# A kernel that plans its own instruction order: new figures in the planner of a fused attention and feed-forward kernel

## The chip, the core and the metric

The kernel runs on one core of a Trainium2 chip. A core has TensorE (matmuls, PE in the profile; its weight loads are PEld), VectorE (DVE), ScalarE (ACT), GpSimd (POOL) and SyncE (SP, which here issues the transfers). Each engine works through its own queue strictly in the order in which the program was written. The metric is the time of one execution on the device, in microseconds (us), the median of several runs.

## The reference

Landmark attention over 8 batches, 8 heads, 576 positions and 64 dimensions, with 32 landmarks, and then a feed-forward layer of 512 to 2048 to 512 with a residual:

```python
q_lm = q.reshape(B, H, 32, 18, D).mean(axis=3)      # k_lm alike
A  = softmax(scale * q @ k_lm.T)                    # 576 x 32
Bm = softmax(scale * q_lm @ k_lm.T)                 # 32 x 32
C  = softmax(scale * q_lm @ k.T)                    # 32 x 576
Z  = Bm.T / (norm1(Bm) * norminf(Bm) + 1e-6)
for _ in range(6):
    Z = 2 * Z - Z @ Bm @ Z
x  = (A @ Z @ C @ v), heads side by side            # 8 x 576 x 512
xn = (x - mean) / sqrt(var + 1e-6) * g_ln
out = x + maximum(xn @ w_ch1, 0) @ w_ch2
```

Inputs and output are float32 in the chip's main memory.

## The kernel before, in words

A batch's heads form two units of four. A unit of q, k or v (576 KB) is loaded by one transfer on SP's queue into a tile `stg` (L247), of which there are six. For batches 1 to 7 GpSimd casts it to half precision: q and k to `nat`, v to `natv` (L796 and following). VectorE transposes `nat` in 32x32 blocks to `xT` and sums it up for the landmarks (`turn`, `add_up`); for some units GpSimd does the sums (`asum`, `s`). TensorE spreads the landmarks (`spread`), ScalarE puts them into `lm`. `attention2` (L876) does the attention of one batch or a pair of batches: scores (`psec`, `psea`), ScalarE's exponentials (`ec`, `ea`), six iterations of the inverse (`iterate`: small matmuls, then one operation on VectorE, `st`), the product with v (`pscv`), and the normalizing of `ea`, for which TensorE sums (`psd`), ScalarE takes logarithm and exponential (`lns`), and GpSimd multiplies. The sets are batch 1, batch 2, batches 3 and 4, batches 5 and 6, batch 7. Batch 0 has a preamble of its own (`attention0`).

The first layer of a batch (`First`, L1093) makes `m16` from the landmark form of A, the values and the first weights, so that the 2048 hidden values of a position come from `ea` by matmuls of 128x288 into `psh`; ScalarE or VectorE evicts them through the relu into `hT`. The second layer multiplies `hT` by the second weights (16 matmuls of 128x512 for each block of 128 positions, into `bank`), and VectorE adds the result, scaled by the deviation `rstd`, to the residual block `xblk`, which SP stores. A batch has four and a half blocks; GpSimd copies the last 64 columns of `hT` of an even batch to the next one's tile (`keep_tail`).

Up to L1406 the order is written out by hand: loads of batches 0 and 1 and all weights, GpSimd's scalings of the first weights (`scale_w1`) and casts of the second (`cast_w2`), and batch 0's attention. From there `run()` (L1340) makes the order. It holds four streams (attentions, first layers, batch 0's residual rows, second layers). A stream gives, at each step, the time from which its next step can start. `run()` takes the first of them that can start now, in that order, or else the one that can start soonest; when the soonest is over 250 ns away and TensorE has had little to do, it puts in a filler matmul (`warm`). Before each step `help_out` (L1268) hands out work to the other queues: stores, the next load, the next cast for GpSimd if GpSimd is believed to be free within 600 ns and the cast's data there, the next job for VectorE if VectorE is believed free within a lead of 400 or 700 ns:

```python
if clock.free["DVE"] <= now + lead():
    mine = [c for c in sets if c.jobs][:1]
```

All this happens while the program is built, not on the chip. What "now" and "free" mean is decided by the class `Clock` (L72): every instruction that is recorded goes through `note` (L122), which reads when its operands are ready, adds a duration from `took` (L108) or from the branch for matmuls or transfers, and moves the engine's `free` forward. The chip never sees these figures, only the order that they make. They also decide which engine evicts: `sooner` (L522) takes ScalarE or VectorE by whichever would end first, and `chunk` (L1126) does so for the relu, with 650 and 810 ns.

The names of tiles are the keys of `note`; the two weight tiles and `hT` are kept in parts (`parted`), and an instruction counts only for the part at its first element (`key_of`, L67).

Of the kernel before, what the change touches and what calls it, by code (L numbers as in the profile page):

```python
# [20 lines left out]
def kernel(  # L21
# [40 lines left out]
    def name_of(x):  # L62
        return x.tensor.name if hasattr(x, "tensor") else x.name

    parted = {}

    def key_of(ap):  # L67

        n = name_of(ap)
        return f"{n}:{ap.offset // parted[n]}" if n in parted else n  # L70

    class Clock:  # L72


        WAY = 55.0

        def __init__(self):
            self.free = dict.fromkeys(("PE", "DVE", "Activation", "Pool", "SP"), 0.0)
            self.wrote, self.used, self.begun = {}, {}, {}
            self.small, self.lanes, self.wire = False, {}, 0.0  # L80
            self.cells, self.count, self.mark, self.fetched = [], 0, 100, 0.0
# [15 lines left out]
        def at(self, *tiles):  # L97
            return max([self.wrote.get(name_of(t), (0.0, ""))[0] for t in tiles] + [0.0]) + self.WAY

        def at_key(self, ap):  # L100
            return self.wrote.get(key_of(ap), (0.0, ""))[0] + self.WAY

        def idle(self, *tiles):

            return max([max(self.wrote.get(n, (0.0, ""))[0], self.used.get(n, (0.0, ""))[0],
                            self.begun.get(n, 0.0)) for n in map(name_of, tiles)] + [0.0]) + self.WAY

        def took(self, i, e, n, m):  # L108
            op = type(i).__name__
            if e == "Activation":  # L110
                return 190 + 0.79 * n
            if e == "Pool":
                return 100 + 0.92 * n if "Copy" in op else 280 + 1.76 * n
            if "Stats" in op:
                return 690 if m > 100 else 180
            if n == 1024:
                return 900
            if "Transpose" in op:
                return 110 + 1.15 * n
            return 140 + 1.15 * max(n, m if "Reduce" in op else 0)  # L120

        def note(self, i):  # L122
            e = str(i.engine).rsplit(".", 1)[-1]
            outs = [a.bass_ap for a in i.outs if hasattr(a, "bass_ap")]
            ins = [a.bass_ap for a in i.ins if hasattr(a, "bass_ap")]
            size = [[k for _, k in a.ap] for a in outs + ins]
            count = []
            for dims in size:
                n = 1
                for k in dims[1:]:  # L130
                    n *= k
                count.append(n)
            ready = 0.0
            for a in ins:
                t, who = self.wrote.get(key_of(a), (0.0, e))
                if who != e:
                    ready = max(ready, t + self.WAY)
            for a in outs:
                for t, who in (self.wrote.get(key_of(a), (0.0, e)), self.used.get(key_of(a), (0.0, e)),
                               (self.begun.get(key_of(a), 0.0), "")):  # L140
                    if who != e:
                        ready = max(ready, t + self.WAY)
            if type(i).__name__ == "InstDMACopy":
                start = max(self.free[e], ready)
                self.free[e] = start + (580 if e == "SP" else 100)
                self.wire = max(start + 1650, self.wire) + count[0] * size[0][0] * 4 / 370.0
                done = self.wire + 600
                start = done
            elif e == "PE":
                cols = count[0]  # L150
                self.count += 1
                if self.count >= self.mark:
                    self.mark += self.BLOCK
                    ready = max(ready, self.fetched)
                    self.fetched = max(self.now(), ready) + self.FETCH
                rows_, cols_ = tuple(i.tile_size)
                self.cells.append((self.now(), cols / 2.4 * rows_ * cols_ / 128 ** 2))
                if tuple(i.tile_size) == (128, 128):
                    if self.small:
                        self.free[e] = max(list(self.lanes.values()) + [self.free[e]]) + 100  # L160
                        self.small, self.lanes = False, {}
                    start = max(self.free[e], ready)
                    self.free[e] = start + max(cols / 2.4 + 3, 56)
                    done = self.free[e] + 160
                else:
                    if not self.small:
                        self.small, self.lanes = True, {}
                        self.free[e] += 100
                    lane = tuple(i.tile_position)
                    start = max(self.free[e], ready, self.lanes.get(lane, 0.0))  # L170
                    self.lanes[lane] = start + max(cols / 2.4, 70)
                    self.free[e] = start + 6
                    done = self.lanes[lane] + 160
            else:
                start = max(self.free[e], ready)
                done = self.free[e] = start + self.took(i, e, count[0], max(count[1:] + [0]))
            for a in ins:
                n = key_of(a)
                self.used[n] = max(self.used.get(n, (0.0, e)), (done, e))
            for a in outs:  # L180
                n = key_of(a)
                self.wrote[n] = max(self.wrote.get(n, (0.0, e)), (done, e))

    clock = Clock()
# [6 lines left out]
    class Ring:  # L191
# [16 lines left out]
        def next(self, tag, k=1):  # L208
# [4 lines left out]
            if any(o in self.pinned for o in olds):  # L213
                return NEVER
            return clock.WAY + max(max(clock.wrote.get(o, (0.0,))[0], clock.used.get(o, (0.0,))[0])
                                   for o in olds)
# [100 lines left out]
    for i in range(NV):  # L317
        t = const.tile([P, U, NJ, 2, D + 1], FP16, name=f"natv{i}")
# [9 lines left out]
    for u in range(U):  # L328
        for nm in ("q", "k"):
            t = nat.tile([P, NJ, 2, D], FP16, name="nat", tag="nat")  # L330
# [149 lines left out]
    heads, ready, multiplied, cast_v = {}, set(), {0}, {0}  # L480
# [957 lines left out]
```

## The time and the profile before

| | |
|---|---|
| time, median of 3 runs | 291.2 us (290.29 to 291.4) |
| the profiled execution, its own time | 291.77 us |
| its span, first to last instruction | 290.0 us |
| mean granted TensorE clock | 0.987 of full |
| TensorE, VectorE, ScalarE, GpSimd busy | 274.0, 187.1, 160.1, 141.7 us |
| moved by transfers | 46.68 MB |
| longest kinds of waits | VectorE for TensorE's `bank` 35.8 us, GpSimd for `lns` 31.6 us |

The span is what the profile's times are counted in; the execution's own time has 1.77 us more around it. A busy time is the time in which an engine had an instruction at work; matmuls are pipelined, so that a busy TensorE need not be TensorE at its peak. An idle engine's wait is put down to the instruction whose end released it. The busiest stretch of the transfers is 7 to 58 us, at 330 to 390 GB/s; behind 152 us hardly anything but stores is moved.

### The profile page before, as it was taken

What the parts mean: (1) busy time and instruction counts of PE and PEld (TensorE: products, weight loads), DVE (VectorE), ACT (ScalarE), POOL (GpSimd) and SP (SyncE); (2) the same over time, 40 slices, a digit from 0 to 9 for tenths busy, and PEclk for the clock granted to TensorE, in tenths of its full rate; (3) what the DMA queues carried; (4) which work ended last, traced back from release to release, by engine and by line L of the source; (5) the groups of instructions that cost most, each with busy time, mean ns of one, the idle gap of its engine ahead of it and who ended that gap; (6) DMA issues with size and microseconds to landing.
All of it is one profiled execution on the core that took longest, in us unless ns stands there. A gap on an engine that the chain in (4) does not pass through costs nothing.

```text
span 290.0 us, 8202 instructions
## 1 busy us (share of the span) xinstructions
PE 274.0 (94%) x3426; PEld 147.9 (51%) x3426; DVE 187.1 (65%) x412; ACT 160.1 (55%) x282; POOL 141.7 (49%) x171
## 2 busy tenths in 40 slices
PE   7888996998899999999889999999999999999994
PEld 7644553345444565444445645556445644564443
DVE  3558975699999875997888284878265373422222
ACT  2567955128851787448889755567277732570000
POOL 4378779899998999999980008400003001000000
PEclk9999999599999999999999999999999999999999
DMA  7999999979545499873800112111120113112333
GB/s 244 381 390 386 387 388 390 299 243 329 168 161 150 133 307 335 240 242 108 287 8 3 36 31 48 39 38 36 41 64 12 37 36 75 37 38 61 80 76 75
DMA packets 23374, 46.68 MB, mean 161 GB/s; under 512 B 2212, under 2 KB 2472, under 8 KB 23336
## 3 DMA queue, kind: packets, MB, share of 16 engines
q1 hardware_dynamic: 23176, 46.02, 49.5%
q8 instruction: 27, 0.44, 0.6%
q10 hardware_dynamic: 160, 0.13, 0.2%
q14 instruction: 11, 0.09, 0.1%
HBM read 36.70 MB, written 9.44 MB: 159 GB/s over the span
## 4 chain that ended last, share of the span: by engine, by line
PE 53%; DVE 14%; POOL 13%; DMA 12%; issue 4%; ACT 1%; SPq 1%; POOLq 0%; DVEq 0%; ACTq 0%
PE bank L240 38%; PE psh L240 12%; DMA stg<-in_v_dram 5%; DMA wstg<-in_moe_w_ch_dram 5%; POOL nat L234 4%; POOL asum L234 3%; POOL natv L234 3%; DVE m L234 2%; DVE six L234 2%; DVE w L234 2%; DMA stg<-in_k_dram 2%; DVE part L234 2%; DVE xblk L234 1%; DVE xT L234 1%; POOL w L234 1%
## 5 line engine op out<-in xcount | busy, mean ns | idle before, releaser
L240 PE MATMUL bank<-w,hT 128*128 128x512 f16 (+1 forms) x592 | 148.5, 379 | 0.5 <-issue 0.5
L240 PEld LDWEIGHTS <-hT 128*128 128x128 f16 x592 | 54.8, 98 | 53.6 <-issue 9.9
L234 ACT ACTIVATE hT<-psh 128x576 f16<-128x576 f32 x111 | 69.0, 651 | 22.3 <-PE psh L240 21.6
L240 PE MATMUL psh<-ea,m 128*128 128x288 f16 x512 | 76.5, 286 | 3.1 <-ACT hT L234 1.8
L240 PEld LDWEIGHTS <-m 128*128 128x128 f16 x512 | 48.6, 98 | 27.6 <-issue 9.4
L234 DVE SCALAR_TENSOR_TENSOR xblk<-bank,rstd,xblk 128x512 f32<-128x512 f32 (+1 forms) x37 | 26.8, 728 | 34.8 <-PE bank L240 34.8
L234 POOL CAST natv<-stg 64x1152 f16<-64x1152 f32 (+1 forms) x23 | 26.7, 1161 | 31.4 <-PE pscv L240 22.4
L234 POOL CAST nat<-stg 128x1152 f16<-128x1152 f32 x28 | 32.5, 1180 | 2.0 <-DMA stg<-in_k_dram 1.1
L234 POOL TENSOR_TENSOR ea<-ea,lns 128x576 f16<-128x576 f16 x14 | 17.8, 1286 | 31.6 <-ACT lns L234 31.6
L234 ACT COPY xblk<-bank 128x512 f32<-128x512 f32 (+1 forms) x34 | 19.0, 595 | 18.5 <-PE bank L240 18.4
L234 DVE BATCH_NORM_STATS2 six<-xblk 128x6 f32<-128x512 f32 x36 | 24.3, 676 | 2.6 <-ACT xblk L234 2.5
L234 DVE STREAM_TRANSPOSE xT<-nat 128x576 uint32<-128x576 uint32 x28 | 21.5, 766 | 2.5 <-POOL nat L234 2.5
L234 ACT CAST m<-bank 128x512 f16<-128x512 f32 x30 | 17.0, 588 | 7.0 <-PE bank L240 7.0
L234 DVE CAST m<-bank 128x512 f16<-128x512 f32 x18 | 12.4, 687 | 12.9 <-PE bank L240 12.8
L234 DVE TENSOR_REDUCE part<-xT 128x32 f16<-128x576 f16 x28 | 20.4, 746 | 0.3
L234 ACT ACTIVATE lns<-psd 128x576 f32<-128x576 f32 x16 | 10.3, 646 | 18.1 <-PE psd L240 15.1
L234 POOL TENSOR_TENSOR asum<-asum 128x256 f32<-128x256 f32 (+1 forms) x28 | 17.2, 615 | 2.2
L234 POOL COPY hT<-hT 128x1024 f16<-128x1024 f16 x4 | 4.2, 1038 | 28.9 <-PE bank L240 28.9
L234 POOL TENSOR_TENSOR asum<-nat 128x512 f32<-128x512 f16 x14 | 16.8, 1202 | 1.1
L234 DVE SCALAR_TENSOR_TENSOR st<-st,bank 128x128 f16<-128x128 f16 (+2 forms) x36 | 11.1, 308 | 7.3 <-PE bank L240 7.3
L240 PE MATMUL bank<-zcbd,ea 128*128 128x256 f16 (+1 forms) x80 | 14.5, 275 | 1.2 <-DVE m L234 0.8
L234 DVE TENSOR_SCALAR hT<-psh 128x576 f16<-128x576 f32 x17 | 12.8, 753 | 4.1 <-PE psh L240 3.6
(114 smaller groups left out, 277.6 us busy)
## 6 DMA issues: line engine op xcount, KB each, us to landing
stg<-in_q_dram SPq DMA_DIRECT2D x16, 576.0 KB, 5.5
stg<-in_k_dram SPq DMA_DIRECT2D x16, 576.0 KB, 5.2
stg<-in_v_dram SPq DMA_DIRECT2D x16, 576.0 KB, 6.2
out_dram<-xblk SPq DMA_DIRECT2D x70, 128.0 KB, 2.3
wstg<-in_moe_w_ch_dram SPq DMA_DIRECT2D x16, 512.0 KB, 7.0
out_dram<-xblk ACTq DMA_DIRECT2D x2, 64.0 KB, 2.1
out_dram<-xblk SPq DMA_DIRECT2D x2, 64.0 KB, 2.2
g_rows<-in_moe_g_ln_dram SPq DMA_DIRECT2D x1, 2.0 KB
```

The lines of the kernel that those rows point to most:

```text
L234: return lambda *args, **kw: keep(getattr(self.engine, op)(*args, **kw))
L240: keep(nc.tensor.matmul(o, l, r, start=start, stop=stop, tile_position=(rb, cb), skip_group_check=(skip or cb != 0)))
```

## The change

The class `Clock` gets other figures; the rest of the file stays. Loads are believed to run at 385 instead of 370 GB/s, and to be complete later the longer they queued (by up to 2200 ns). Copies of 1152 elements on VectorE are believed to take 760 ns, casts and operations of 512 to 576 elements 100 + 1.13 n. GpSimd's scaling with a per-partition factor gets 100 + 1.29 n instead of 280 + 1.76 n. ScalarE, VectorE and GpSimd are believed free for the next instruction 110, 80 and 30 ns before an instruction's end, while an instruction that reads a result of its own engine still counts it from its end. Matmuls on a part of the array occupy each 32x32 cell that they cover, for at least 30 instead of 70 ns, with 4 or 8 instead of 6 ns between two. The fetching of instructions takes 3000 instead of 4300 ns where no transfer is under way. And an instruction counts for every part of a parted tile that it touches. The order of the instructions that `run()` makes follows from these figures.

```diff
+    def keys_of(ap):
         n = name_of(ap)
-        return f"{n}:{ap.offset // parted[n]}" if n in parted else n
+        if n not in parted:
+            return [n]
+        at = [ap.offset]
+        for step, k in list(ap.ap)[1:]:
+            if step >= parted[n]:
+                at = [o + step * i for o in at for i in range(k)]
+        return [f"{n}:{o // parted[n]}" for o in at]
...
+        OVERLAP = {"Activation": 110, "DVE": 80, "Pool": 30}
...
             if e == "Pool":
+                if "Ptr" in op:
+                    return 100 + 1.29 * n
                 return 100 + 0.92 * n if "Copy" in op else 280 + 1.76 * n
+            if n == 1152 and "Copy" in op:
+                return 760
             if "Stats" in op:
                 return 690 if m > 100 else 180
+            if n >= 512 and (n == 576 or op == 'InstTensorCopy'):
+                return 100 + 1.13 * n
...
-                if who != e:
-                    ready = max(ready, t + self.WAY)
+                if who != e or e != "PE":
+                    ready = max(ready, t + (self.WAY if who != e else 0.0))
...
-                self.wire = max(start + 1650, self.wire) + count[0] * size[0][0] * 4 / 370.0
-                done = self.wire + 600
+                self.wire = max(start + 1650, self.wire) + count[0] * size[0][0] * 4 / 385.0
+                done = self.wire + 600 + min(2200, 0.6 * (self.wire - start - 1650))
...
-                    self.fetched = max(self.now(), ready) + self.FETCH
+                    self.fetched = max(self.now(), ready) + (self.FETCH if self.wire > self.now() else 3000)
...
-                        self.free[e] += 100
-                    lane = tuple(i.tile_position)
-                    start = max(self.free[e], ready, self.lanes.get(lane, 0.0))
-                    self.lanes[lane] = start + max(cols / 2.4, 70)
-                    self.free[e] = start + 6
-                    done = self.lanes[lane] + 160
+                        self.free[e] += 95
+                    lane = [(a, c) for a in range(i.tile_position[0], i.tile_position[0] + rows_, 32)
+                            for c in range(i.tile_position[1], i.tile_position[1] + cols_, 32)]
+                    start = max([self.free[e], ready] + [self.lanes.get(x, 0.0) for x in lane])
+                    self.lanes.update((x, start + max(cols / 2.4, 30)) for x in lane)
+                    self.free[e] = start + (8 if rows_ == 64 and cols < 128 else 4)
+                    done = self.lanes[lane[0]] + 160
             else:
                 start = max(self.free[e], ready)
-                done = self.free[e] = start + self.took(i, e, count[0], max(count[1:] + [0]))
+                done = start + self.took(i, e, count[0], max(count[1:] + [0]))
+                self.free[e] = done - self.OVERLAP[e]
...
```

## The prediction

> **What bounds the kernel now.** I read the page first, then the busy time by stretch, then the timeline around the one place where the clock digit falls, then GpSimd's timeline. From the page:
>
> ```profile
> span 290.0 us, 8202 instructions
> PE 274.0 (94%) x3426; PEld 147.9 (51%) x3426; DVE 187.1 (65%) x412; ACT 160.1 (55%) x282; POOL 141.7 (49%) x171
> PE   7888996998899999999889999999999999999994
> PEclk9999999599999999999999999999999999999999
> POOL 4378779899998999999980008400003001000000
> ```
>
> TensorE is busy 94% of the span, so an order can win only its holes and the slow slice: the eighth slice (50.8 to 58.0 us) ran at half clock. GpSimd is full to about 150 us and nearly empty behind it. The busy times by stretch (columns: busy us and count of PE, PEld, DVE, ACT, POOL; granted clock; DMA share; GB/s):
>
> ```profile
> 44.00:48.00 4.00, 4.00 (x147) 1.81 (x131) 2.31 (x9) 2.67 (x4) 3.46 (x4) 1.00 1.06 393
> 48.00:51.20 3.20, 0.55 (x25) 0.20 (x15) 1.82 (x4) 1.33 (x2) 3.20 (x4) 0.85 1.06 389
> 51.20:55.00 3.80, 3.80 (x21) 1.31 (x25) 2.60 (x7) 0.00 (x0) 3.48 (x6) 0.50 0.99 334
> 55.00:59.00 4.00, 4.00 (x43) 1.30 (x42) 2.66 (x6) 1.33 (x2) 3.22 (x4) 0.74 0.96 280
> 98.00:131.00 33.00, 32.29 (x586) 17.02 (x583) 26.43 (x60) 21.08 (x38) 31.12 (x35) 1.00 0.79 262
> 131.00:138.00 7.00, 6.48 (x73) 3.46 (x73) 5.47 (x12) 6.21 (x13) 6.75 (x6) 1.00 0.43 119
> 138.00:151.00 13.00, 11.21 (x99) 6.47 (x99) 11.51 (x27) 10.77 (x20) 12.23 (x14) 1.00 0.50 160
> 181.00:286.00 105.00, 104.90 (x907) 56.10 (x905) 49.14 (x98) 45.82 (x83) 7.11 (x6) 1.00 0.21 48
> ```
>
> Between 48 and 51.2 us TensorE works 0.55 us of 3.2; then its clock is 0.50 for 3.8 us and 0.74 for 4 us. From 181 us on it has no hole at all: 104.90 of 105. What happens at 48 us:
>
> ```profile
> 48.16 3.33 POOL L234 CAST nat<-stg 128x1152 f16<-128x1152 f32 x3
> 49.34 0.78 DVE L234 STREAM_TRANSPOSE xT<-nat 128x576 uint32<-128x576 uint32 x1 [2.54 <-POOL nat L234]
> 50.15 0.75 DVE L234 TENSOR_REDUCE part<-xT 128x32 f16<-128x576 f16 x1
> 50.82 0.28 DVE L234 SCALAR_TENSOR_TENSOR st<-st,bank 128x128 f16<-128x128 f16 x1
> 51.16 0.29 PE L240 MATMUL bank<-st 32*32 32x64 f16 x8 [2.65 <-DVE st L234]
> ```
>
> VectorE runs in the order in which the builder recorded its work. A transpose of batch 2's tile (xT) stands there ahead of batch 1's iteration (st). Its input comes from GpSimd's cast at 49.31, VectorE waits 2.54 us, and the iteration, whose products were in the bank at 47.15, is done at 51.1. TensorE has everything else behind that iteration and waits 2.65 us. The builder put the transpose first because, as I read help_out, it believed VectorE busy until the cast was there. Last, GpSimd between 117 and 134 us:
>
> ```profile
> 117.75 3.33 POOL L234 CAST nat<-stg 128x1152 f16<-128x1152 f32 x3
> 124.11 1.14 POOL L234 CAST nat<-stg 128x1152 f16<-128x1152 f32 x1
> 128.29 2.54 POOL L234 TENSOR_TENSOR ea<-ea,lns 128x576 f16<-128x576 f16 x2
> 131.06 2.54 POOL L234 TENSOR_TENSOR ea<-ea,lns 128x576 f16<-128x576 f16 x2 [0.23 <-ACT lns L234]
> ```
>
> Casts and sums for batches 5 and 6 (117.75 to 128.29) stand ahead of the normalizing of batches 3 and 4 (ea). The chain of waits runs through GpSimd here, from 98 to 132 us.
>
> **The change part by part.** It adds and removes no kind of work: every matmul, cast, load and store stays. Up to the call of run() the order is written out by hand, so SP's loads, GpSimd's scalings and casts and VectorE's first casts stand as before, and the first 24 us or so are the same. In run() three things can move: who goes first in each queue (SP's stores against its loads, GpSimd's casts against ea, VectorE's xT and part against st, ScalarE's evictions), which of ScalarE and VectorE takes an eviction, and where filler matmuls stand (none were put in by run() before: the zeros' full-array matmuls end at 23 us).
>
> *Copies of 1152 on VectorE.* Believed 140 + 1.15 x 1152 = 1465 ns, the row has 760, and the new figure is 760. Four casts at the start: 4 x 0.705 = 2.8 us of belief taken off VectorE (less where a load is the later). *Overlap.* Two evictions of hT of 0.65 us take 1.19 together on ScalarE (row at 66.76), so 0.11 is shared; the new model takes 110 ns off there and 80 on VectorE. Both move the believed TensorE and VectorE earlier against GpSimd. The 2.8 us alone is the size of the 2.54 us wait.
>
> *GpSimd's scaling.* Believed 280 + 1.76 x 512 = 1181, row 756, new 100 + 1.29 x 512 = 760: 12 x 0.42 = 5.1 us off. It speaks against the change, since GpSimd would now be believed earlier too; but GpSimd waits before nearly every cast from 33 to 45 us for its load (the waits have 4.9 us on weights, 8.1 on v), so loads set its time there. *Loads.* 370 to 385 GB/s: 576 KB in 1.53 us instead of 1.59; and up to 2.2 us more until a queued load counts as landed. The two about cancel after 26 loads (26 x 0.06 = 1.5 against at most 2.2), so GpSimd is believed where it was, give or take 1 us. Price if wrong: a transpose let in early again, up to 2.65 us.
>
> *Small products* (70 to 30 ns, 6 to 4 or 8 between two) and *parts of tiles*: neither has a wait of its own in the trace. A burst of 8 st products is believed 40 ns sooner; batch 0's odd rows of the second weights get a due time, while TensorE shows no wait for w casts from 36 to 43 us, where second-layer products first run beside these casts. I take 0 for both, cover: TensorE itself. If the cover is gone, 6 iterations in 5 sets x 40 ns = 1.2 us, either sign. *Evictions that change engine*: 646 ns on ScalarE against 753 on VectorE, x17 went to VectorE; ten that change are 10 x 0.11 = 1.1 us either way; I take 0, both engines having holes behind 98 us.
>
> *What the hole is worth.* TensorE: 2.65 us idle, and the clock: 3.8 x 0.50 + 4.0 x 0.26 = 2.9 us; 5.6 us in all. [...]
>
> *What of it reaches the end.* After 131 us TensorE is full, so the end moves only as far as batches 3 and 4 are ready sooner, or as TensorE enters that stage with less left to do. Left of batch 2's second layer at 131.7 us: 10 matmuls of 128x512, 10 x 0.216 = 2.2 us (a row of seven takes 1.68 us and of one 0.38: 1.30 / 6 = 0.216). An early TensorE can do these before; beyond that it waits for ea. And ea: its first lns is there at about 126.5 us (ScalarE's log at 125.2, 0.65 + 0.68), GpSimd comes to it at 128.29: up to 1.8 us, if casts for 5 and 6 count as ready later and stand behind. I take half of it: 2.2 + 0.9 = 3.1 us. Ends: 0 (nothing carried) and the whole 5.6 + 1.8 = 7.4; from below, see the second rival.
>
> [...] From 74.7 to 85.8 us VectorE runs eight two-input additions on the weights (w<-w,less), and GpSimd's casts beside them take 1.60 instead of 1.14 us, its sums 1.48 instead of 1.16: 2 casts x 0.46, 2 sums x 0.32 and 4 smaller ones x 0.33, 2.9 us lost. [...] I take 0 and let 2.9 us stand in the range.
>
> Sum: span 290.0 - 3.1 = 286.9; with the profiled execution's 1.77 around it (291.77 - 290.0) 288.7; the median of the runs is 0.57 below the profiled one, so 288.1 us.
>
> **The rivals.** *GpSimd swallows it.* It is at work from 43.15 to 133.6 us with waits of 0.41, 0.70 and 0.81 and gaps of 0.08; if its order stays, batches 3 and 4 are ready when they were, and TensorE merely waits from 126 to 132 us. For it: the chain through GpSimd. Against: the 2.2 us of leftover work. Time: 290.2 to 291.2.
>
> *Casts are put off* (slower). The later landing keeps a cast out of GpSimd's queue although its data is there; help_out finds GpSimd free only in steps of TensorE's clock, and GpSimd, full from 57 to 134 us, gets holes. Eighteen tiles are cast or normalized in 98 to 134 us; 0.3 us lost on each is 5.4 us. It decides from the point where GpSimd's new holes exceed the 2.2 us of leftover; 5.4 - 2.2 = 3.2 us: 294.4 us. For it: 31.12 of 33 us busy, so every hole counts, and the 2.9 us of contention that the model leaves out. Against: GpSimd's waits for loads in that stretch are nil now, so many casts could come later without harm.
>
> *It does nothing*: the moved beliefs cancel and the order is nearly the same: 291.2 us. Against it, 2.8 us on VectorE is larger than the lead of 0.4 us that help_out uses.
>
> **How the numbers follow.** About 0.5% is what a measurement of this kernel tells from none: 289.7 and 292.7 are the bounds. Hole closed and carried: 0.47, all faster, own range 284 to 289.7, 288.1 its value. Swallowed: 0.15 (0.03 faster, 0.09 same, 0.03 slower). Put off: 0.35 (0.02 same, 0.33 slower, up to 297). Nothing: 0.03. Together faster 0.50, same 0.14, slower 0.36. The range 283.8 (the whole 7.4) to 295.2 (put off, and 0.8 of the contention with it) leaves out about 2 in 10, most of it at the slow end.
>
> **What would show it.** Right: no VectorE wait of over 1 us for nat near 48 us; no half-clock slice after 45 us; st's iterations of batch 1 done by about 54 us (before: 60); batches 3 and 4's last ea before 133 us; full TensorE from then on. Wrong: a GpSimd idle of over 2 us in 57 to 134 us; the half-clock slice at another place; the same hole with another tile; or filler matmuls of zeros behind 24 us.

## The result, and the profile after

The kernel with the new figures takes 293.68 us (median of 4 runs, 292.83 to 295.15); the kernel before took 290.98 us beside it. The ratio is 1.0100 with a 95% interval of 1.0055 to 1.0146: slower by 2.9 us of 291.2, where 3.1 us less were predicted. The profiled execution of after took 295.15 us, the longest of its four. In after's profile the helper lines are L252 and L258 (before: L234 and L240). From its page:

```profile
span 293.4 us, 8208 instructions
PE 274.4 (94%) x3428; PEld 147.9 (50%) x3428; DVE 184.1 (63%) x406; ACT 163.4 (56%) x288; POOL 141.0 (48%) x171
PE   7888999989799899979989999999989999999994
POOL 4377878999999999967990017400003000000000
PEclk9999999999999999979999999999999999999999
```

The slow slice at 51 us is gone. Another one stands further right: the 18th (124.7 to 132.0 us, clock digit 7), in which GpSimd also drops to 6. The same stretches as before (columns: busy us and count of PE, PEld, DVE, ACT, POOL; granted clock; DMA share; GB/s):

```profile
48.00:51.20 3.20, 3.20 (x38) 1.36 (x31) 2.63 (x8) 2.55 (x4) 2.61 (x4) 1.00 1.05 390
51.20:55.00 3.80, 3.80 (x46) 1.45 (x45) 3.72 (x10) 0.27 (x1) 3.72 (x4) 1.00 0.98 351
98.00:131.00 33.00, 29.58 (x551) 15.11 (x551) 23.88 (x54) 16.91 (x30) 30.24 (x34) 0.96 0.78 251
131.00:138.00 7.00, 7.00 (x74) 3.54 (x73) 5.53 (x13) 5.14 (x10) 4.38 (x4) 0.92 0.16 37
181.00:286.00 105.00, 104.19 (x886) 54.26 (x885) 44.48 (x91) 47.63 (x89) 9.12 (x8) 1.00 0.21 49
```

TensorE works 3.20 of 3.20 us where it worked 0.55, at full clock. In exchange it works 2.7 us less in 98 to 131 us (29.58 after 32.29). VectorE at the old hole:

```profile
48.57 0.28 DVE L252 SCALAR_TENSOR_TENSOR st<-st,bank 128x128 f16<-128x128 f16 x1
49.35 0.29 DVE L252 SCALAR_TENSOR_TENSOR st<-st,bank 128x128 f16<-128x128 f16 x1 [0.50 <-PE bank L258]
49.56 0.77 DVE L252 STREAM_TRANSPOSE xT<-nat 128x576 uint32<-128x576 uint32 x1
```

The transpose now stands behind two more iterations and waits for nothing. Batch 1's zt is there at 53.4 us (before: 61.2), its first layer begins at 56.9 (63.6). What follows, first TensorE, then GpSimd:

```profile
124.92 1.04 PE L258 MATMUL bank<-w,hT 128*128 128x512 f16 x4
128.15 3.10 PE L258 MATMUL bank<-w,hT 128*128 128x512 f16 x8 [2.19 <-issue]
131.05 0.69 PE L258 MATMUL psd<-ea,bones 128*128 128x288 f16 x2
```

```profile
123.18 1.14 POOL L252 CAST nat<-stg 128x1152 f16<-128x1152 f32 x1
...
127.36 2.52 POOL L252 TENSOR_TENSOR ea<-ea,lns 128x576 f16<-128x576 f16 x2
133.27 1.29 POOL L252 TENSOR_TENSOR ea<-ea,lns 128x576 f16<-128x576 f16 x1 [3.40 <-ACT lns L252]
134.84 1.28 POOL L252 TENSOR_TENSOR ea<-ea,lns 128x576 f16<-128x576 f16 x1 [0.28 <-ACT lns L252]
```

TensorE stands 2.19 us with "issue" as the releaser: no engine and no load that the profile knows held it. The sums psd for the second pair of ea come at 131.05 (before: 128.59), ScalarE's lns late with them, GpSimd waits 3.40 us, and the last ea of batches 3 and 4 is done at 136.1 us (before: 133.6). The first layer of batch 3 begins at 136.9 (134.6), and TensorE's last matmul ends at 289.7 (286.2).

To see where the won time went, I took each stage's length less the time that its matmuls need at 2.4 columns per ns on the whole array, the planner's own figure (the rows show 2.37, 0.216 us for 512 columns; I counted parts of the array in proportion, and filler matmuls of zeros not at all). It is TensorE's lost time, in us, by stage, worked out from the traces; three rows belong to experiments below. The stages are cut at fixed times, so that work which moves across a cut moves its losses too.

| stage, us | 24–44 | 44–59 | 59–77 | 77–98 | 98–112 | 112–131 | 131–152 | 152 to end | sum |
|---|---|---|---|---|---|---|---|---|---|
| before | 3.4 | 8.4 | 4.9 | 5.0 | 1.2 | 5.8 | 7.1 | 15.3 | 50.9 |
| after | 3.6 | 3.8 | 6.5 | 5.1 | 2.4 | 8.6 | 7.5 | 16.8 | 54.4 |
| short_loads | 3.6 | 3.8 | 6.5 | 5.1 | 2.4 | 5.9 | 7.9 | 15.6 | 51.0 |
| c16_short | 3.6 | 4.0 | 6.1 | 3.7 | 2.3 | 5.9 | 7.9 | 14.9 | 48.4 |
| before_short | 4.4 | 5.2 | 5.3 | 5.0 | 1.2 | 6.7 | 7.6 | 15.4 | 50.9 |

After wins 4.6 us at 44 to 59, as the hole promised, and gives back 1.7 at 59 to 77, 1.3 at 98 to 112, 2.8 at 112 to 131 and 1.5 behind 152. These are several places, and so the experiments ask for more than one cause.

### The profile page after: what moved, and what is told of

It reads as the page before. It is cut to its first block, busy times and chain, and to the rows that moved or that the text cites. A ratio compares the mean times of both kernels' runs of the same rounds, so it can differ in the third digit from the quotient of the medians.

```text
span 293.4 us, 8208 instructions
## 1 busy us (share of the span) xinstructions
PE 274.4 (94%) x3428; PEld 147.9 (50%) x3428; DVE 184.1 (63%) x406; ACT 163.4 (56%) x288; POOL 141.0 (48%) x171
## 4 chain that ended last, share of the span: by engine, by line
PE 65%; DVE 18%; issue 5%; ACT 4%; POOL 4%; DMA 3%; SPq 0%; POOLq 0%; ACTq 0%; DVEq 0%
PE bank L258 43%; PE psh L258 18%; DMA stg<-in_q_dram 3%; DVE xT L252 3%; DVE w L252 3%; DVE part L252 2%; DVE xblk L252 2%; DVE m L252 2%; ACT lns L252 1%; DVE st L252 1%; PE psd L258 1%; POOL natv L252 1%; PE pscv L258 1%; DVE six L252 1%; POOL asum L252 1%
## 5 line engine op out<-in xcount | busy, mean ns | idle before, releaser
L258 PE MATMUL bank<-w,hT 128*128 128x512 f16 (+1 forms) x592 | 145.0, 377 | 2.8 <-issue 2.2
L258 PEld LDWEIGHTS <-hT 128*128 128x128 f16 x592 | 55.3, 98 | 55.7 <-issue 10.2
L252 ACT ACTIVATE hT<-psh 128x576 f16<-128x576 f32 x116 | 72.4, 651 | 18.2 <-PE psh L258 17.1
L258 PE MATMUL psh<-ea,m 128*128 128x288 f16 x512 | 77.6, 286 | 3.1 <-ACT hT L252 1.3
L258 PEld LDWEIGHTS <-m 128*128 128x128 f16 x512 | 47.8, 97 | 28.4 <-issue 9.7
L252 DVE SCALAR_TENSOR_TENSOR xblk<-bank,rstd,xblk 128x512 f32<-128x512 f32 (+1 forms) x37 | 26.8, 728 | 46.2 <-PE bank L258 46.1
L252 POOL CAST natv<-stg 64x1152 f16<-64x1152 f32 (+1 forms) x23 | 26.7, 1159 | 29.8 <-PE pscv L258 20.7
L252 POOL TENSOR_TENSOR ea<-ea,lns 128x576 f16<-128x576 f16 x14 | 17.7, 1284 | 36.9 <-ACT lns L252 36.9
L252 POOL CAST nat<-stg 128x1152 f16<-128x1152 f32 x28 | 32.5, 1177 | 2.1 <-DMA stg<-in_k_dram 1.1
L252 ACT COPY xblk<-bank 128x512 f32<-128x512 f32 (+1 forms) x34 | 19.0, 588 | 22.1 <-PE bank L258 21.9
L252 DVE BATCH_NORM_STATS2 six<-xblk 128x6 f32<-128x512 f32 x36 | 24.3, 675 | 10.1 <-ACT xblk L252 10.1
L252 ACT CAST m<-bank 128x512 f16<-128x512 f32 x30 | 17.0, 587 | 10.0 <-PE bank L258 9.9
L252 DVE STREAM_TRANSPOSE xT<-nat 128x576 uint32<-128x576 uint32 x28 | 21.5, 768 | 1.1 <-POOL nat L252 0.9
L252 DVE TENSOR_REDUCE part<-xT 128x32 f16<-128x576 f16 x28 | 20.3, 744 | 0.3
L252 ACT ACTIVATE lns<-psd 128x576 f32<-128x576 f32 x16 | 10.3, 644 | 18.2 <-PE psd L258 18.2
L252 DVE CAST m<-bank 128x512 f16<-128x512 f32 x18 | 12.3, 682 | 12.5 <-PE bank L258 12.5
L252 POOL TENSOR_TENSOR asum<-asum 128x256 f32<-128x256 f32 (+1 forms) x28 | 17.5, 626 | 2.2
L252 POOL COPY hT<-hT 128x1024 f16<-128x1024 f16 x4 | 4.1, 1037 | 29.7 <-PE bank L258 25.3
L252 POOL TENSOR_TENSOR asum<-nat 128x512 f32<-128x512 f16 x14 | 16.8, 1200 | 1.1
L258 PE MATMUL bank<-zcbd,ea 128*128 128x256 f16 (+1 forms) x80 | 13.8, 275 | 1.5 <-DVE m L252 0.8
L252 DVE SCALAR_TENSOR_TENSOR st<-st,bank 128x128 f16<-128x128 f16 (+2 forms) x36 | 11.0, 306 | 6.5 <-PE bank L258 6.5
L258 PE MATMUL bank<-w,zt 64*32 64x512 f16 x256 | 14.2, 386 | 0.5 <-ACT less L252 0.4
```

Source lines behind the costliest of these rows:

```text
L252: return lambda *args, **kw: keep(getattr(self.engine, op)(*args, **kw))
L258: keep(nc.tensor.matmul(o, l, r, start=start, stop=stop, tile_position=(rb, cb), skip_group_check=(skip or cb != 0)))
```

## The experiments

Ratios are to the kernel before on the same chip, with 95% intervals. The expectations use these names. Theory A: the lead at 48 us is real, and GpSimd or later stages take it back. B: one group of figures spoils the order. C: any small shift of the figures changes the order at random by about 1%. M: the old figures, too long for what they describe, were a margin that covered losses for which no figure stands.

### One group of figures at a time

VectorE's copies and its operations of 512 to 576 elements alone:

```diff
+            if n == 1152 and "Copy" in op:
+                return 760
...
+            if n >= 512 and (n == 576 or op == 'InstTensorCopy'):
+                return 100 + 1.13 * n
```

> The kernel before with the new figures for VectorE's copies and operations of 512 to 1152 elements alone. Theory A (the lead won near 48 us is real, but GpSimd and the later stages take it back): the hole at 48 us closes, batch 1's zt comes before 57 us (before 61.2), and the time stays within 2 us of before, 289 to 293. Theory B (one group of figures by itself makes the bad order): 293 or more only if this is the group. Theory C (the order is so sensitive that any small change of figures moves the time by 1 per cent either way): 288 to 295 with no tie to zt.

Measured: 0.9949 (0.9923 to 0.9976), faster than both kernels. Batch 1's zt comes at 58.3 us in it; TensorE's hole is still there, with 1.50 us at 51.0.

The overlap alone (OVERLAP taken off `free`, an own result counted from its end):

```diff
-                done = self.free[e] = start + self.took(i, e, count[0], max(count[1:] + [0]))
+                done = start + self.took(i, e, count[0], max(count[1:] + [0]))
+                self.free[e] = done - self.OVERLAP[e]
```

> The kernel before with the overlap on ScalarE, VectorE and GpSimd alone. Theory A: the believed TensorE runs earlier too, the hole at 48 us shrinks by half or more, time 289 to 293. Theory B: 293 or more if the overlap is the group that makes the order worse (its stages are believed 5 to 6 us shorter in sum). Theory C: anything from 288 to 295.

Measured: 1.0047 (1.0023 to 1.0070). The old hole shrinks to 0.66 us, and another opens at 77.5 us, 1.73 us for VectorE's st.

The small products alone (cells instead of lanes, 30 instead of 70 ns):

```diff
-                    self.lanes[lane] = start + max(cols / 2.4, 70)
-                    self.free[e] = start + 6
+                    self.lanes.update((x, start + max(cols / 2.4, 30)) for x in lane)
+                    self.free[e] = start + (8 if rows_ == 64 and cols < 128 else 4)
```

> The kernel before with the new figures for small products alone. Theory A: little, 290 to 293, the hole at 48 us stays, since these figures hardly touch VectorE against GpSimd before 48 us. Theory B: 293 or more if the cheap small products make TensorE's believed clock run ahead of the instruction fetch and of GpSimd. Theory C: anything from 288 to 295.

Measured: 0.9987 (0.9958 to 1.0015), no difference that can be told. It closes the hole at 48 us as fully as the whole change (3.8 us lost at 44 to 59), and nothing of that can be told at the end. It is not the hole alone, though: TensorE stands 1.53 us at 125.0 us with "issue" in this order too, where before stands 0.53.

The loads alone (385 GB/s, later landing in a queue):

```diff
-                self.wire = max(start + 1650, self.wire) + count[0] * size[0][0] * 4 / 370.0
-                done = self.wire + 600
+                self.wire = max(start + 1650, self.wire) + count[0] * size[0][0] * 4 / 385.0
+                done = self.wire + 600 + min(2200, 0.6 * (self.wire - start - 1650))
```

> The kernel before with the new figures for loads alone. Loads are believed to land up to 2.2 us later, so VectorE's and GpSimd's work on them is laid later. Theory M: a margin is added, none taken away; the hole at 48 us grows or stays, 290 to 292. Theory B (the later landing spoils GpSimd's order): 293 or more.

Measured: 0.9992 (0.9973 to 1.0011), no difference that can be told. GpSimd's scaling alone and the parts of tiles alone gave the very instructions of the kernel before, so neither was run. The sixth group, 3000 instead of 4300 ns for the fetching of instructions, does change the order when it is put in alone; it was run neither alone nor left out.

### The change without one group

> The whole change without the overlap: ScalarE, VectorE and GpSimd are again believed busy to each instruction's end, a margin of 80 to 110 ns each. Theory M (the old figures' overcharges were a margin that covered what no figure counts, the contention with GpSimd and the instruction fetch): much of the loss comes back, 289.5 to 292. Theory B (another group makes the order worse): 293 to 294.

Measured, whole change with the old `free`: 1.0075 (1.0049 to 1.0101). TensorE stands 2.51 us up to 127.05, again with "issue".

> The whole change without the new figures for small products, 70 ns and 6 ns as before. Theory M: TensorE is believed slower in the attentions and part of the loss comes back, 290.5 to 292.5. Theory B with the overlap as the culprit: 293 to 294.

Measured, whole change with the old small products: 1.0120 (1.0096 to 1.0143). No hole at 128 us here, but 7.7 us lost at 77 to 98 (before 5.0).

The single groups make -0.5, +0.5, -0.1 and -0.1%, which add up to -0.2; all groups in one kernel make +1.0, and leaving out the harmful overlap doesn't bring it back. For the two groups that were left out B falls, and so does M. The change without the copies, the loads or the figure for the fetch was not run, so the loss isn't shown to be independent of these.

### Is the order a lottery?

WAY, the time from one engine's end to another's start, 56 instead of 55 ns in before; 60 in after:

```diff
-        WAY = 55.0
+        WAY = 56.0
```

> The kernel before with the figure for a handover between engines 56 instead of 55 ns, nothing else: no better and no worse an estimate, but the order of TensorE, VectorE and ScalarE differs in places, GpSimd's and SP's do not. Theory A and B: within 0.5 per cent of before, 289.7 to 292.3. Theory C: outside this.

Measured: 1.0003 (0.9981 to 1.0025), although the order changed on TensorE, VectorE and ScalarE.

> The changed kernel with 60 instead of 55 ns for a handover, which changes the order of all engines in places. Theory A and B: within 0.5 per cent of the changed kernel, 292.2 to 295.1. Theory C: outside this, either way.

Measured: 1.0028 (1.0007 to 1.0049), 0.7% better than after. TensorE's idle time near 128 us is 1.56 instead of 2.19 us. A shift so small can be worth 0.7%, but before's order moved without a change in time; C is neither shown nor excluded as a part of it.

> The changed kernel once more, timed beside its parts on one chip: 293 to 294.5 by every theory; a profiled execution without the half-clock stretch near 130 us has a span about 1.5 us under the first one's 293.4.

The change itself once more: 1.0096 (1.0060 to 1.0132). In its profile, of an execution of 297.76 us, TensorE stands 2.43 us up to 130.7, in front of the same matmul as in after.

### Contention put into the figures

```diff
+                if e == "DVE" and count[0] == 1024:
+                    self.crowd.append((start, done))
+                if e == "Pool":
+                    done += 0.42 * sum(max(0.0, min(done, b) - max(start, a)) for a, b in self.crowd[-8:])
```

and 1060 instead of 900 ns for VectorE's long additions.

> The changed kernel with the centring of the weights and its effect on GpSimd put into the figures: 1060 instead of 900 ns for the eight additions of 1024 on VectorE, and GpSimd's work 0.42 longer for the share that lies beside them. Theory A: the believed and the real time of GpSimd stay together behind 80 us, the order for batches 3 and 4 is laid for the real GpSimd, and 1 to 3 us come back: 291 to 292.5. Theory B: no change, 293 to 294, since the wrong figure is another one. Theory C: 288 to 296, no tie to GpSimd.

Measured: 1.0066 (1.0035 to 1.0098); after's own interval covers it. Telling the planner of the loss brings nothing that can be told.

### The long additions cut down

VectorE centres the first weights in eight additions of 128x1024. Here they work on 16 of 512 columns, and the planner still counts them full, so that the order is exactly after's (and before's); most of the weights are left uncentred:

```diff
-        dve.tensor_tensor(out=o, in0=o, in1=less(f)[:, None, :].broadcast_to([P, 2, 512]),
+        o = w1_16[:, ds(c, 2), ds(512 * f, 16)]
+        dve.tensor_tensor(out=o, in0=o, in1=less(f)[:, None, 0:16].broadcast_to([P, 2, 16]),
```

> The changed kernel in exactly its order, with the eight centring additions on VectorE cut from 512 to 16 columns (14 of 15 parts of that addition are left out, so the first layer's weights stay uncentred), while the builder still counts them in full. Theory A: GpSimd's casts and sums beside them take their usual 1.15 us, GpSimd is 3 us earlier behind 85 us, and as GpSimd gates batches 3 and 4 the whole ends 2 to 4 us earlier than the changed kernel, 290 to 291.5. Against it (TensorE and the evictions gate): under 1 us, 293.

> The kernel before in exactly its order, with the same eight additions cut to 16 columns (the weights stay uncentred). Theory A: less than in the changed kernel, 0 to 2 us, since in its order GpSimd has a wait of 0.8 us at 94 us and second-layer work is left to cover it: 289 to 291. If the contention costs both orders alike, 2 to 4 us: 287 to 289, and then it does not tell the two apart.

Measured: after's order 0.9962 (0.9940 to 0.9984), before's 0.9958 (0.9939 to 0.9978). Without the additions the two orders take the same time. The cut is worth 1.4% in after and 0.4% in before. But the idle time at the fetch had also shrunk, to 0.97 us, so two causes could be mixed here; c16_short below parts these two. What no run parts: the cut takes away the time that GpSimd loses beside the additions, and also 5.8 us of VectorE's own work (12.7 to 6.9 us in 57 to 100 us, all operations that read `less`).

### GpSimd does ea before the casts for 5 and 6

```diff
-                if c.casts:
+                if c.casts and not holding[0]:
```

with `holding[0]` set while ea of batches 3 and 4 wait to be normalized.

> The whole change; added to it, GpSimd gets no further cast from the end of batches 3 and 4's product with v until their ea are normalized, so the casts and sums for batches 5 and 6 come behind these. Theory G (the won lead is lost because GpSimd works for 5 and 6 ahead of ea of 3 and 4): last ea of batches 3 and 4 by about 132 us instead of 136.1, first layer of batch 3 begins by about 133 instead of 136.9, ratio to before 0.995 to 1.002. Theory T (TensorE's own holes around 126 to 132 us and the contention before them hold the stage; GpSimd only waits for lns): GpSimd's work moves, ea stays at 134 us or later, ratio 1.005 to 1.012. In both, casts for 5 and 6 end some 3 us later, which TensorE can hide only if it has second-layer work left.

Measured: 1.0058 (1.0036 to 1.0080), 0.4% better than the change. Its profile (291.7 us, one of its shorter executions) has the last ea at 130.5 us and batch 3's first layer at 131.2, as theory G said; the time lies between the two theories. TensorE's idle time with "issue" is 0.85 us in it, since the order moved too, so it doesn't tell G from T.

### The loads in front of TensorE's fetch

In the trace of after a transfer of 16 KB on the queue named "instruction" starts at 118.65 us and the next at 125.79; TensorE goes on 1.4 us after the end of the latter. 27 such transfers (the page's q8, 0.44 MB) stand against 6856 instructions of TensorE (3428 matmuls and as many weight loads), one for every 254, and so I take them for TensorE's code. The other runs' traces bear this out: in 15 of the 20 profiles TensorE stands idle, for 0.31 to 2.51 us, in front of its 1760th matmul, whatever that matmul is in the order at hand, and goes on 1.1 to 1.5 us after the end of such a transfer. In copies_and_loads, for one, it is a psd, in after a second-layer matmul:

```profile
125.88 0.28 PE L244 MATMUL psd<-ea,bones 128*128 128x288 f16 x1 [1.11 <-issue]
```

Two other long idle times with "issue" lie 128 and 256 matmuls before it (1.46 us in copies_and_loads, 1.03 in after_crowd), with their weight loads about one and two transfers' worth of instructions. The same count in so many orders leaves little but the fetch as the cause. The five without it are the three with short loads (short_loads, before_short, c16_short), but_small and only_overlap.

SP's four loads of v of batch 6 and k of batch 7 lie between the two transfers. This experiment keeps after's exact order and cuts these four:

```diff
+            if (nm, b) in (("v", 6), ("k", 7)):
+                t = stage.tile([P, 2, NJ, D], FP32, name="stg", tag="stg")
+                keep(queue.dma_start(out=t[:, :, 0:1, :], in_=...[:, :, 0:1, :]))
...
+                whole = stg[:, :, 0:1, :].to_broadcast([P, 2, NJ, D])
```

> The whole change in its exact order; only the loads of v of batch 6 and k of batch 7 (four units of 576 KB, on the wire about 117 to 126 us) fetch one position in nine, which the casts then read nine times; the planner still counts whole units. So the values of batch 6 and the keys of batch 7 are other numbers. Theory F (TensorE's idle time of 2.19 us at 128 us is its instruction fetch queued behind these loads): the idle time falls to under 1 us, no half clock behind it, batches 3 and 4's last ea by about 133 us; ratio to before 1.000 to 1.004, 2 to 3 us better than the change. Rival (the fetch takes that long anyway, or the hole has another cause): idle time of over 1.5 us stays, ratio 1.007 to 1.012.

Measured: 1.0021 (1.0004 to 1.0039). 1.0100 - 1.0021 is 0.8%, 2.3 us. The two stretches around the hole, after first, then short_loads:

```profile
124.00:128.20 4.20, 2.00 (x25) 0.63 (x24) 4.17 (x8) 1.33 (x2) 3.88 (x6) 1.00 0.97 344
128.20:132.00 3.80, 3.80 (x12) 1.52 (x13) 1.91 (x4) 0.17 (x1) 1.68 (x2) 0.56 0.10 26
```

```profile
124.00:128.20 4.20, 4.19 (x36) 1.86 (x35) 4.17 (x8) 1.33 (x2) 3.88 (x6) 1.00 0.29 66
128.20:132.00 3.80, 3.49 (x54) 1.55 (x53) 3.73 (x10) 2.82 (x5) 3.57 (x4) 1.00 0.37 84
```

VectorE, ScalarE and GpSimd do the same amount in the first stretch; only TensorE differs, 2.00 against 4.19 us, with 344 against 66 GB/s moved by the DMA engines, and only after has the clock at 0.56 behind it. TensorE and GpSimd of short_loads:

```profile
124.93 2.76 PE L259 MATMUL bank<-w,hT 128*128 128x512 f16 x12
127.53 0.41 PE L259 MATMUL psd<-ea,bones 128*128 128x288 f16 x2
```

```profile
127.39 2.54 POOL L253 TENSOR_TENSOR ea<-ea,lns 128x576 f16<-128x576 f16 x2
130.16 2.54 POOL L253 TENSOR_TENSOR ea<-ea,lns 128x576 f16<-128x576 f16 x2 [0.23 <-ACT lns L253]
```

The twelve second-layer matmuls run through, psd is there 3.5 us earlier than in after, GpSimd waits 0.23 instead of 3.40 us and is done with ea at 132.7 (136.1). From there to the end short_loads is ahead by as much: the last matmul ends at 286.2 (289.7). And the transfer: the instruction queue in 121 to 128.2 us, after and then short_loads (count, MB, share of 16 engines):

```profile
q8 instruction: 1, 0.02, 0.8%
```

```profile
q8 instruction: 2, 0.03, 1.8%
```

The one that after has at 125.79 starts at 122.02 in short_loads, so the loads had held it up by about 3.8 us. Theory F holds. The control, the same cut in before's exact order:

> The kernel before in its exact order, with the same four loads (v of batch 6, k of batch 7) cut to one position in nine, so the values of batch 6 and keys of batch 7 are other numbers. Theory F (in the new order TensorE's fetch waits behind these loads; in the old one it loses only 0.53 us there): at most 0.5 us less, ratio 0.998 to 1.000. Rival (shorter loads help any order, through memory or GpSimd, and say nothing of the fetch): ratio 0.990 to 0.994, as much as the 2.3 us that they brought in the new order.

Measured: 0.9998 (0.9976 to 1.0020). Shorter loads bring nothing that can be told to the old order, which lost only 0.53 us at its fetch.

### Both cuts in the new order

> The whole change in its exact order with both cuts: the weights are centred in 16 of 512 columns only (so without most of VectorE's eight long additions beside GpSimd; the first weights stay uncentred elsewhere), and the four loads fetch one position in nine. The cut of the centring alone gave 0.9962 and had the idle time at the fetch at 0.97 us instead of 2.19; the cut of the loads alone 1.0021. If contention and fetch are two losses that add (3.9 and 2.3 us): 0.988 to 0.990. If most of what the centring's cut brought was the shorter hole at the fetch: 0.994 to 0.997, and contention is then worth about 1.5 to 2 us, not 3.9.

Measured: 0.9904 (0.9872 to 0.9935). The losses add, nearly: 1.0021 - 0.9904 = 1.2%, 3.4 us for the additions with the fetch out of the way. How they cost so much, from GpSimd's rows in short_loads and in c16_short, which differ in the additions alone:

```profile
70.08 1.92 POOL L253 TENSOR_TENSOR asum<-asum 128x256 f32<-128x256 f32 x2
72.08 0.75 POOL L253 TENSOR_TENSOR s<-asum,nat 128x128 f16<-128x128 f32 x1
72.78 1.60 POOL L253 CAST nat<-stg 128x1152 f16<-128x1152 f32 x1
74.46 1.47 POOL L253 TENSOR_TENSOR asum<-nat 128x512 f32<-128x512 f16 x1
```

```profile
70.13 1.26 POOL L253 TENSOR_TENSOR asum<-asum 128x256 f32<-128x256 f32 x2
71.47 0.43 POOL L253 TENSOR_TENSOR s<-asum,nat 128x128 f16<-128x128 f32 x1
71.84 1.14 POOL L253 CAST nat<-stg 128x1152 f16<-128x1152 f32 x1
73.06 1.16 POOL L253 TENSOR_TENSOR asum<-nat 128x512 f32<-128x512 f16 x1
```

GpSimd waits for nobody in either; its own instructions are longer beside the additions (0.66, 0.32, 0.46, 0.31 us here, then 0.34, 0.47 and 0.32 us to 81 us: 2.9 us). Its last ea of batches 3 and 4 is 2.8 us later for it (132.7 against 129.9), TensorE's end 2.7 us. The additions also hold up TensorE directly: five of them stand on VectorE ahead of an st, and this wait is gone in c16_short. In after:

```profile
69.63 5.31 DVE L252 TENSOR_TENSOR w<-w,less 128x1024 f16<-128x1024 f16 x5
75.58 0.19 PE L258 MATMUL bank<-st,bones 128*128 128x64 f16 x1 [1.13 <-DVE st L252]
```

In before the additions cost GpSimd 2.9 us too: it is 3.5 us later at the end of its s at 87.4 us (83.9 with the cut), of which 0.6 was there before the first addition. At ea only 1.8 us are left. The next wait says why, in before and in c16_before:

```profile
94.34 0.43 POOL L234 TENSOR_TENSOR s<-asum,nat 128x128 f16<-128x128 f32 x1 [0.81 <-DVE sT L234]
```

```profile
92.61 0.43 POOL L234 TENSOR_TENSOR s<-asum,nat 128x128 f16<-128x128 f32 x1 [2.60 <-DVE sT L234]
```

In the old order GpSimd waits there for VectorE anyway, and 2.60 - 0.81 = 1.8 us of the delay is absorbed. The new order has no such wait, and nothing absorbs it.

### A part of the change

> VectorE's figures for copies and 512 to 576 elements alone, again, with more rounds: 0.995 if the first measurement holds, 1.000 if it was luck.

Measured: 0.9938 (0.9917 to 0.9959).

> VectorE's figures for copies and 512 to 576 elements together with the loads' figures, the rest as before. If gains of single groups add: 0.9949 x 0.9992 = 0.994. If any further figure spoils the order as in the whole change: 1.000 to 1.010. I take 0.997.

Measured: 0.9931 (0.9909 to 0.9953), 290.07 against 291.64 us: the best kernel here, 2.0 us by the ratio, though not to be told from copies alone. In both GpSimd does ea of batches 3 and 4 ahead of the last cast for batch 6, which the old order has the other way round; the four rows in copies_again:

```profile
123.46 2.54 POOL L238 TENSOR_TENSOR ea<-ea,lns 128x576 f16<-128x576 f16 x2 [0.21 <-ACT lns L238]
126.50 1.28 POOL L238 TENSOR_TENSOR ea<-ea,lns 128x576 f16<-128x576 f16 x1 [0.50 <-ACT lns L238]
129.52 1.28 POOL L238 TENSOR_TENSOR ea<-ea,lns 128x576 f16<-128x576 f16 x1 [1.74 <-ACT lns L238]
130.75 1.14 POOL L238 CAST nat<-stg 128x1152 f16<-128x1152 f32 x1
```

The last ea is done at 130.8 us (before: 133.6), although TensorE stands 1.75 us at its fetch in this order. That GpSimd's order is the gain was not tried alone. The hole at 48 us isn't the gain: the profile of copies_again still has it, TensorE 0.75 of 3.20 us, and copies_and_loads, no faster by what can be told, has none. The stretches of copies_again:

```profile
48.00:51.20 3.20, 0.75 (x77) 0.62 (x76) 1.10 (x3) 0.04 (x1) 3.20 (x4) 1.00 1.06 394
51.20:55.00 3.80, 3.80 (x41) 1.75 (x38) 3.73 (x11) 2.67 (x4) 3.48 (x5) 1.00 0.78 229
```

## Why the prediction was wrong

**Right: the place.** The transpose moved behind the iterations, VectorE's wait of over 1 us for nat went, the iterations of batch 1 were done at 52.6 us (forecast: about 54), and the stage won 4.6 us (forecast: 5.6, clock included). Parts of tiles and GpSimd's scaling at 0 were right, and small products and loads at 0 too, each alone.

**The step that failed: "What of it reaches the end".** It carried 3.1 us to the end, 2.2 of leftover second-layer work and 0.9 of an earlier ea. The runs show nothing carried and 2.9 us lost. short_loads, the new order without its idle time at the fetch, is the clearest: it wins the 4.6 us at the hole, its ea is done 0.9 us earlier than in before, the size that the sum had, and its last matmul ends at 286.2 us as in before, with a ratio of 1.0021. By its table row the lead goes at 59 to 77 us (1.7), 98 to 112 (1.3), 131 to 152 (0.8) and in small parts elsewhere. At 98 us TensorE waits for VectorE, and VectorE had waited for GpSimd (the rows are after's; in short_loads the waits are 0.92 and 1.34 us):

```profile
98.08 0.24 DVE L252 STREAM_TRANSPOSE sT<-s 128x64 uint32<-128x64 uint32 x1 [0.91 <-POOL s L252]
98.70 0.38 PE L258 MATMUL bank<-part,spread 128*128 128x256 f16 x2 [1.32 <-DVE part L252]
```

The step rested on "After 131 us TensorE is full", and the prediction's own rows say otherwise: 6.48 of 7.00 us in 131 to 138 and 11.21 of 13.00 in 138 to 151, 2.3 us of holes in which work done early meets new waits. Only from 152 us on is before full.

**The rival *GpSimd swallows it*** is half borne out. Part of the lead goes in waits behind GpSimd, and in the new order GpSimd brings ea only 0.9 us earlier, but batches 3 and 4 aren't ready "when they were". In before_short, before's own order with a hole that happened to be 1.08 us, ea is done 1.4 us earlier (132.2); TensorE then has half clock for 3.4 us from 131.7 us, and ends at 286.3. The time of this rival, 290.2 to 291.2, lies just under what the change would take without the fetch: 1.0021 x 291.2 = 291.8, the interval reaching from 291.3 to 292.3.

**The terms that were missing.** *The fetch*: no row of the prediction's working held it, though before's TensorE had its 0.53 us in the trace and the diff a figure for it. It is 2.3 us. *Contention* (GpSimd's instructions that are longer beside the additions), "I take 0 and let 2.9 us stand in the range": the loss on GpSimd was rightly sized at 2.9, and 0 would be right if it reached the end alike in both orders; in the old one 1.8 us of it had been hidden by the wait for sT. Cutting the additions wins 3.4 us in the new order and 0.42%, 1.2 us, in the old: 2.2 us more. This is for the additions as a whole; that GpSimd's loss is most of it is argued from the 2.8 us at ea and 2.7 at the end. Set against these two, 0.9904 - 0.9958 = -0.54%, 1.6 us, is what the new order is worth with both out of the way (the old order with both cuts was not run; its shorter loads alone brought nothing that can be told). That -1.6 + 2.2 + 2.3 gives the measured +2.9 us proves nothing, since the three are differences of the same ratios, with intervals of some 0.2 to 0.5% each.

**The loss beside the additions** showed in the new order as in before's rows: 1.60 us for a cast beside the additions, 1.14 without them (short_loads, c16_short). No figure of the planner counts it, so believed GpSimd was too early behind this place. But in after_crowd (1.0066, the change 1.0100) a figure for it in the planner brought no gain that can be told.

**The clock.** The prediction took 2.9 us of slower clock behind before's hole as won with the hole, from one profile. One was too little. TensorE's wait for st at 50 to 51 us and the granted clock from 51.2 to 55 us were 2.65 us and 0.50 in before, 2.72 and 0.65 in only_loads, 2.22 and 0.70 in c16_before, 2.18 and 0.58 in before_way56, but 2.45 and 1.00 in copies_again (the two rows above). What brings the slower clock was not shown. The 2.9 us of clock were an upper end. Of 231 executions of before beside the experiments, the 44 with a mean granted clock of 0.997 or more took 290.4 us in the median, the 110 at 0.993 to 0.996 took 291.7, the 61 under 0.99 took 292.5. At 0.997 or more the five of after and after_again took 293.3 us, short_loads 291.8 (18 executions), c16_before 289.4 (4) and c16_short 289.1 (5). At equal clock, then, the new order is 1.4 us behind even without its fetch, and about even when the additions are cut too: most of the 1.6 us above goes with the clock, and the 2.65 us of the hole itself brought nothing that can be told. Some of these groups are small, and they come from several chips.

**The slower rival, *Casts are put off*,** had the sign and nearly the time (294.4), and not the mechanism. Three of the signs named for being wrong came: half clock at another place (128.7 us), filler matmuls of zeros behind 24 us (two, at 142 and 144 us), and an idle time of GpSimd of over 2 us. But this last is one of 3.40 us for lns, behind TensorE, and no cast with its data there stands waiting. GpSimd's rows from 57 to 126 us are without a hole.

**What stays open.** Of what after loses more at 59 to 77 and 98 to 112 us, TensorE's wait of 1.13 us for st belongs to the additions and the one of 1.32 for part comes through GpSimd; but c16_short still has most of the loss of both stages (6.1 and 2.3 us), so these waits are not all of it. Why but_small is slow without idle time at its fetch was not pursued, nor what the figure for the fetch does to the order.

## What to carry to other kernels

A hole in the bounding engine is worth at the end only what the queues behind it let through (here 4.6 us were won at the hole and none of it came to the end): follow the next scarce one (here GpSimd, full from 43 to 134 us in before) to the point where it hands over, and look for the holes that the bounding engine still has behind that point, before counting the first hole. When an order gets tighter, look for what the old order's waits had been hiding: a wait of GpSimd for VectorE, 2.60 us long without the additions and 0.81 with them, covered 1.8 us of GpSimd's own slowness. And count instructions, not only work: TensorE had 6856 here, and a transfer that I take for a part of their code began 3.8 us late behind the loads. The sign of it was idle time at the same count in different orders, here in front of the 1760th matmul in 15 of 20 profiles.

## What the hardware showed that I had not expected

TensorE's code seems to come as 16 KB transfers, one for about every 254 of its instructions, each taking 0.88 to 1.82 us in after; behind four queued loads of 576 KB one began 3.8 us late (125.79 against 122.02 us in short_loads), and TensorE stood 2.19 to 2.51 us (after, after_again, but_overlap), against none with the loads cut to a ninth. In 15 of 20 profiles of many orders it stood in front of its 1760th matmul. Behind its 2.19 us the granted clock was 0.56 for 3.8 us in the profile of after; with idle times of 1.53 to 1.75 us at the same place (only_small, after_way60, copies_again) the pages have clock digits of 9 in all slices, and means of 1.00, 0.999 and 1.00. VectorE's additions of two fp16 inputs (128x1024) took 0.83 to 1.63 us in before, and GpSimd's cast of 128x1152 beside them 1.60 instead of 1.14 us.
